# The first block of a fused attention and two-layer kernel, laid by hand on all engines

## The chip, the cores and the metric

The kernel runs on one core of one Trainium2 chip. The metric is device time of one execution, in microseconds (us).

Five engines of the core matter. TensorE (PE in the profile) multiplies matrices; its weight loads are listed apart as PEld. ScalarE (ACT) and VectorE (DVE) do elementwise work and are the only two of the four others that read the matrix results in PSUM here. GpSimd (POOL) does elementwise work on SBUF. SyncE (SP) issues the DMAs. Each engine works through its own instructions in the order in which they were written into its queue; an instruction that waits holds all that stand behind it.

## The reference, cut to what matters

Three stages follow each other on 3072 tokens of 512 features. The first is attention in chunks of 32 queries:

```python
scores = scale * np.matmul(q_c, k_full.transpose(0, 1, 3, 2))
scores = scores - np.max(scores, axis=-1, keepdims=True)
a = np.exp(scores)
a = a / (np.sum(a, axis=-1, keepdims=True) + 1e-09)
out[:, :, c_start:c_end] = np.matmul(a, v_full)
```

The second is a wide layer with a squared ReLU, from 512 to 2048 features and back:

```python
h = x @ w_in
r = np.maximum(h, 0.0)
g = s * (r * r) + b
return (g @ w_out).astype(np.float32)
```

The third is a soft mixture of eight experts. The change touches only the first part of the first two stages.

## The kernel before

The tokens are worked in six blocks of 512. A block needs four attention units (two heads each, numbered u = 0 to 23 over all blocks) and then the wide layer. The 2048 hidden features are cut into 16 slices, and a step n of the first two blocks handles one slice of one block: `divmod(n, 16)` gives block and slice. Steps 0 to 15 are block 0, steps 16 to 31 block 1; later blocks are computed in another way and are not touched.

**One step on TensorE.** `mm_h(n)` is 12 matmuls of 128x512 that make the hidden slice in a PSUM bank (`HB[n % 2]`), `mm_y(n)` is 12 that add the slice's share to four output banks. Products are made from a high and a low part of each operand, three products for each pair. TensorE's order is written by hand: mm_h(n), then an attention piece if the step has one, then mm_y(n-1). Attention pieces are `qk` (32 matmuls: scores), `tr` (4 transposes) and `pv` (32 matmuls: the weighted values). Units 4 to 9 fall in steps 1 to 15: qk in steps 1, 3, 7, 11, 12 and 14, tr in 4, 5, 9, 13 and 14, pv in 5, 7, 11 and 15.

**One step on the other engines.** `make_r` (L362, ScalarE) is the ReLU out of PSUM, `make_t` (L366, VectorE) the square, `make_high` (L369, ScalarE) and `make_low` (L373, VectorE) the two parts of g that mm_y reads. The weights of slice n stand in a tile W[n], first half for mm_h and second half for mm_y. `split_wi` makes the two parts that mm_h reads: `wi_high` (L328, ScalarE) and `wi_low` (L332). `split_wo` does the same for mm_y: `wo_high` (L343, ScalarE) and `wo_low` (L347).

**Decoding.** The weights come in as 8-byte numbers and are turned into 4-byte ones in halves of 128x512, 32 in all. A half is a load into one of up to 11 staging tiles (sp, yt, y), then `w_clamp` (L303, VectorE), `w_begin` (L309 and L310, ScalarE) and `w_end` (L316, VectorE), which writes the half into W and frees the staging tile. `halves` fixes their order: first half of slice n+1, then second half of slice n.

**Attention on the other engines.** `att_exp` is two memsets, a reduction (L220) and a subtraction (L221) on VectorE and the exponential (L222) on ScalarE. `att_norm` is a reduction (L226), two tiny operations (L227, L228) and a multiply of 128x512 (L229). `att_place` copies transposes out of PSUM (L244 and L246 on ScalarE; with the second on VectorE, L248, from unit 8 on). After pv, ScalarE copies (L259) and VectorE makes the low part (L271, `att_low`).

**What sets the order.** The string START is a list of tokens that lays the start by hand on every engine, up to the first steps: q, k, v, w, c are loads, S and A the score work of units 0 to 3, d, e, E the three parts of decoding, H mm_h(0), R, t, g, l the four parts of g(0), I, i and O, o the splits. After it, `plain_step` writes the steps; there the orders of TensorE and SyncE are as written, and those of ScalarE, VectorE and GpSimd come from a scheduler that places instructions by its own estimates. The last four steps of block 1 (`hand_step`) and what follows are laid by hand on these three too. In `plain_step` a step decodes two halves as early as the scheduler sees fit.

Of the kernel before, what the change touches and what calls it, by code (L numbers as in the profile page):

```python
# [27 lines left out]
START = (  # L28
# [4 lines left out]
)  # L33
WSCALE = 256.0
PARTS = ((0, 128), (128, 128), (256, 128), (384, 128))
# [6 lines left out]
def tile_attention_moe_softmoe(  # L42
# [35 lines left out]
    def fresh(name):  # L78
        cur[name] = slot(name, "n")
        return cur[name]  # L80
# [58 lines left out]
    def r32(ap):  # L139
        return ap.bitcast(F32R)  # L140
# [138 lines left out]
    def w_load(most=99):  # L279
        while stage_free and hnext[0] < len(halves) and most:  # L280
            most -= 1
            f, h = halves[hnext[0]]
            hnext[0] += 1
            t = stage_free.pop(0)
            sp.dma_start(out=t.bitcast(U32), in_=wd[f][:, 512 * h:512 * h + 512].bitcast(U32))
            stage_full.append((f, h, t))
# [33 lines left out]
    def w_decode():  # L320
        w_clamp()
        w_begin()
        w_end()
# [5 lines left out]

    def wi_low(n):  # L330
        t, raw = hl(WI[n % 2]), W[n % NF][:, 0:512]
        (dve if n < NF else pool).tensor_tensor(out=r32(t[:, 1]), in0=raw, in1=t[:, 0], op=ALU.subtract)  # L332

    def split_wi(n):
        wi_high(n)
        wi_low(n)
# [12 lines left out]
    def split_wo(n):  # L349
        wo_high(n)  # L350
        wo_low(n)

    def mm_h(n, kts):
        w = WI[n % 2].rearrange("p (a k c) -> p a k c", a=2, k=4)
        for kt in kts:
            x = hl(X[(n // NF) % 2][kt])
            for i, (a, b) in enumerate(((0, 0), (0, 1), (1, 0))):
                pe.matmul(HB[n % 2], lhsT=r32(w[:, a, kt, :]), rhs=r32(x[:, b]),  # L358
                          start=(kt == 0 and i == 0), stop=(kt == 3 and i == 2))
# [841 lines left out]
    with tc.manual_schedule(engines={mybir.EngineType.PE, mybir.EngineType.SP}):  # L1201
# [30 lines left out]
        def s_pv(u):  # L1232
# [29 lines left out]
            "o": wo_low,  # L1262
            "y": lambda _: stage_free.__setitem__(slice(None), YT + stage_free + Y),
        }
        with tc.manual_schedule(engines={mybir.EngineType.Activation, mybir.EngineType.DVE, mybir.EngineType.Pool}):
            for token in START.split():
                steps[token[0]](int(token[1:]))
        w_decode()
        w_decode()
        w_load()  # L1270


        def plain_step(n):
            j, f = divmod(n, NF)
            if 1 < n < NSTEP - 1:
                split_wi(n + 1)
            split_wo(n)
            mm_h(n, (0, 1, 2, 3))
            make_r(n)
            make_g(n)  # L1280
            if n + 2 < NF:
                w_decode()
                w_decode()
                w_load()
            if n == NF - 1:
                for h in range(NHP):
                    fresh(f"x0{h}")
            for task, a in bg[n]:
                run_bg(task, a, None if task == "csoft" else HB[(n + 1) % 2] if task == "pv" and n >= NF - 4 else mbank())
            if 3 <= n < NF + 3:  # L1290
                w_store(n - 3)
            if n:
                mm_y(n - 1)
                if f == 0:
                    y_evac()
            if n >= NF:
                sp.dma_start(out=DWS[f], in_=WO[n % 2])
                for fn, op, kt in XT.get(f, ()):
                    fn(op, 0, kt)
# [44 lines left out]
                w_split(2, 0)  # L1344
                ws_load(R[2], NPR + 1)

        for n in range(1, NSTEP - 4):
            plain_step(n)
        with tc.manual_schedule(engines={mybir.EngineType.Activation, mybir.EngineType.DVE, mybir.EngineType.Pool}):
            for n in range(NSTEP - 4, NSTEP):  # L1350
# [253 lines left out]
```

## Time and profile before

| | us |
|---|---|
| median of 3 runs | 657.0 (656.27 to 657.42) |
| profiled execution, time | 658.39 |
| profiled execution, span from first to last instruction | 656.6 |
| TensorE busy | 640.1 (97% of the span) |
| VectorE busy | 440.8 (67%) |
| ScalarE busy | 355.1 (54%) |
| GpSimd busy | 199.5 (30%) |

The mean granted TensorE clock is 0.995 of full speed. The span begins at the first instruction and ends with the last; 1.8 us of the profiled time lie outside it. In a timeline row the first number is the start in us from the beginning of the span, the second the time from the start of the first to the end of the last instruction in the row; "x12" is the count, and square brackets hold the engine's idle time before the row and what ended it. Matmuls overlap, so 12 of them that take 2.88 us are followed by the next 12 some 2.72 us after their start.

### The profile page before, as it was taken

How to read it: one execution, taken by the hardware profiler on the slowest of the kernel's cores; microseconds unless marked ns; L12 is line 12 of the kernel's file. 1: busy time of each engine (PE TensorE's matmuls, PEld its weight loads, DVE VectorE, ACT ScalarE, POOL GpSimd, SP SyncE). 2: the span in 40 equal slices, each digit the busy share in tenths (PEclk: the TensorE clock that was granted, in tenths of full speed). 3: DMA queues.
4: the chain of work that ended last, by engine and by line, in shares of the span. 5: the costliest groups of instructions: out<-in, count | busy, mean ns of one | idle time of the engine just before them, and what ended most of it. 6: DMA issues, size and time to landing. Idle time of an engine off the chain costs nothing.

```text
span 656.6 us, 12822 instructions
## 1 busy us (share of the span) xinstructions
PE 640.1 (97%) x4965; PEld 512.1 (78%) x4965; DVE 440.8 (67%) x748; ACT 355.1 (54%) x637; POOL 199.5 (30%) x182
## 2 busy tenths in 40 slices
PE   7899999999999999999999999999999999999995
PEld 7687888888878887888788887887887887886384
DVE  5898998566775567755575686715766879566233
ACT  5799895555654465544455464425654455544232
POOL 5100000333443485544334202444455516000000
PEclk9999999999999999999999999999999999999999
DMA  8999956476554856787655586479998788999997
GB/s 327 335 409 367 357 196 211 150 255 216 182 188 140 323 209 229 293 293 287 251 211 193 195 305 218 179 213 364 325 351 316 243 293 315 370 391 409 407 408 309
DMA packets 60108, 184.37 MB, mean 281 GB/s; under 512 B 6672, under 2 KB 6928, under 8 KB 60048
## 3 DMA queue, kind: packets, MB, share of 16 engines
q1 hardware_dynamic: 60048, 183.56, 76.9%
q8 instruction: 39, 0.64, 0.4%
q14 instruction: 21, 0.17, 0.1%
HBM read 137.40 MB, written 46.14 MB: 280 GB/s over the span
## 4 chain that ended last, share of the span: by engine, by line
PE 90%; DVE 5%; DMA 2%; ACT 2%; issue 1%; SPq 0%; DVEq 0%; ACTq 0%
PE bank L388 27%; PE bank L718 22%; PE bank L358 12%; PE bank L974 11%; PE bank L255 3%; PE bank L206 3%; PE bank L1459 2%; PE bank L1418 2%; PE bank L440 2%; PE bank L235 1%; DMA yt<-wd 1%; PE bank L414 1%; PE bank L456 1%; PE bank L1488 1%; DMA k<-kd 1%
## 5 line engine op out<-in xcount | busy, mean ns | idle before, releaser
L388 PE MATMUL bank<-g,wo 128*128 128x512 f32 x528 | 132.0, 400 | 2.0 <-ACT g L369 2.0
L388 PEld LDWEIGHTS bank<-g,wo 128*128 128x128 f32 x528 | 97.8, 190 | 24.1 <-ACT g L369 2.1
L358 PE MATMUL bank<-x,wi 128*128 128x512 f32 x384 | 92.2, 389 | 0.0
L358 PEld LDWEIGHTS bank<-x,wi 128*128 128x128 f32 x384 | 72.1, 188 | 15.0
L332 POOL TENSOR_TENSOR wi<-w,wi 128x512 fp32r<-128x512 f32 x16 | 21.1, 1319 | 121.0 <-ACT wi L328 112.0
L366 DVE SCALAR_TENSOR_TENSOR rt<-bank,cons,rt 128x512 f32<-128x512 f32 x32 | 23.9, 747 | 32.4 <-ACT rt L362 32.4
L347 POOL TENSOR_TENSOR wo<-w,wo 128x512 fp32r<-128x512 f32 x16 | 21.9, 1368 | 47.4 <-ACT wo L343 38.8
L328 ACT ACTIVATE wi<-w 128x512 fp32r<-128x512 f32 x32 | 20.1, 628 | 20.8 <-PE bank L358 18.9
L710 POOL TENSOR_TENSOR w14n<-sp6n,w14n 128x512 fp32r<-128x512 f32 x8 | 14.6, 1826 | 47.5 <-ACT w14n L709 47.5
L373 DVE SCALAR_TENSOR_TENSOR g<-rt,cons,g 128x512 fp32r<-128x512 f32 x32 | 24.2, 756 | 6.5 <-ACT g L369 6.4
L255 PEld LDWEIGHTS bank<-pb,v 128*64 128x64 f32 x704 | 22.3, 138 | 7.9 <-issue 3.3
L343 ACT ACTIVATE wo<-w 128x512 fp32r<-128x512 f32 x32 | 20.0, 626 | 15.4 <-PE bank L388 12.0
L369 ACT ACTIVATE g<-rt,cons 128x512 fp32r<-128x512 f32 x32 | 23.1, 720 | 9.9 <-DVE rt L366 9.7
L255 PE MATMUL bank<-pb,v 128*64 128x64 f32 x704 | 25.3, 225 | 0.5 <-ACT pb L246 0.5
L206 PE MATMUL bank<-k,q 128*64 128x64 f32 x704 | 24.7, 223 | 1.0 <-DMA k<-kd 1.0
L222 ACT ACTIVATE ep<-ep 128x512 f32<-128x512 f32 x22 | 13.8, 629 | 21.7 <-DVE ep L221 21.6
L206 PEld LDWEIGHTS bank<-k,q 128*64 128x64 f32 x704 | 22.4, 138 | 3.3 <-issue 2.2
L733 ACT ACTIVATE rt1n<-y1n 128x1024 f32<-128x1024 f32 x8 | 8.5, 1059 | 29.6 <-DVE y1n L834 29.6
L362 ACT ACTIVATE rt<-bank 128x512 f32<-128x512 f32 x32 | 18.8, 587 | 6.4 <-PE bank L358 6.3
L226 DVE TENSOR_REDUCE ast<-ep 128x8 f32<-128x512 f32 x22 | 15.0, 684 | 8.8 <-ACT ep L222 8.3
L974 PE MATMUL bank<-g,yt0n 128*128 128x512 f32 x72 | 18.6, 396 | 0.2 <-DVE sp L407 0.2
L964 POOL TENSOR_TENSOR k0n<-sp5n,k0n 128x512 fp32r<-128x512 f32 x6 | 8.2, 1360 | 31.9 <-ACT k0n L963 31.8
(688 smaller groups left out, 1691.8 us busy)
## 6 DMA issues: line engine op xcount, KB each, us to landing
v<-vd SPq DMA_DIRECT2D x22, 512.0 KB, 5.6
sp<-wd SPq DMA_DIRECT2D x22, 512.0 KB, 9.6
q<-qd SPq DMA_DIRECT2D x20, 512.0 KB, 6.4
dws<-wo SPq DMA_DIRECT2D x16, 512.0 KB, 5.7
k<-kd SPq DMA_DIRECT2D x22, 332.0 KB, 6.8
wo<-dws SPq DMA_DIRECT2D x12, 512.0 KB, 4.2
dwi<-w SPq DMA_DIRECT2D x16, 256.0 KB, 6.8
dwr<-w SPq DMA_DIRECT2D x16, 256.0 KB, 6.8
```

Source lines behind the costliest of these rows:

```text
L206: pe.matmul(S[64 * par:64 * par + 64, 2 * i + z, :], lhsT=qt[:, c].rearrange("p h n -> p (h n)"), rhs=kt[:, KG * c:KG * c + 64], start=Tru ...
L255: pe.matmul(b[64 * h:64 * h + 64, 64 * m:64 * m + 64], lhsT=vt[:, m, h, :], rhs=pb[:, m // 2, m % 2, h].rearrange("p z n -> p (z n)"), sta ...
L328: act.activation(out=r32(t[:, 0]), in_=raw, func=AF.Copy)
L332: (dve if n < NF else pool).tensor_tensor(out=r32(t[:, 1]), in0=raw, in1=t[:, 0], op=ALU.subtract)
L347: (dve if n < NF else pool).tensor_tensor(out=r32(t[:, :, 1]), in0=raw, in1=t[:, :, 0], op=ALU.subtract)
L358: pe.matmul(HB[n % 2], lhsT=r32(w[:, a, kt, :]), rhs=r32(x[:, b]), start=(kt == 0 and i == 0), stop=(kt == 3 and i == 2))
L366: dve.scalar_tensor_tensor(out=t, in0=HB[n % 2], scalar=s_col, in1=r, op0=ALU.mult, op1=ALU.mult)
L369: act.activation(out=r32(hl(G[n % 2])[:, 0]), in_=hl(RT[n % 2])[:, 1], func=AF.Identity, bias=b_col)
L373: dve.scalar_tensor_tensor(out=r32(g[:, 1]), in0=t, scalar=b_col, in1=g[:, 0], op0=ALU.add, op1=ALU.subtract)
L388: pe.matmul(yb[dt], lhsT=r32(w[:, dt // 2, a, dt % 2 * 128:dt % 2 * 128 + 128]), rhs=r32(g[:, b]), start=(first and i == 0), stop=(last an ...
L718: pe.matmul(b, lhsT=r32(wv[:, a, kt, :]), rhs=r32(xv[:, c]), start=(first and kt == 0 and i == 0), stop=(kt == 1 and i == 2), skip_group_c ...
L974: pe.matmul(banks[d], lhsT=r32(w[:, a, d * 128:d * 128 + 128]), rhs=r32(g[:, b]), start=(first and i == 0), stop=(last and i == 2), skip_g ...
```

## The change

Block 0's steps 1 to 15 are no longer written by `plain_step` but by a new function `first_step`, in which the order on ScalarE, VectorE and GpSimd is fixed by hand as well. Within it, in a step n with n + 1 < 16: mm_h(n); make_r; clamp, begin and end of the half (slice n, second half); make_t between the clamp and the begin; the attention matmuls; after the end mm_y(n-1), make_high, clamp of the half (slice n+2, first half), make_low, the copies of a transpose, begin, att_exp, end; then split_wo(n), split_wi(n+2), att_norm and the stores. So a half is decoded one step ahead of the split that reads it. `wi_low` goes to GpSimd from n = 2 on (before: from n = 16 on), and the multiply of att_norm for units 4 to 9 goes to GpSimd (before: VectorE). START ends earlier (E3, I2, i2 and the two decodes after it are gone, now in step 1) and loads two more staging tiles before q4 and one right after it.

```diff
@@ -28,8 +28,8 @@
-    "k4 q4 c1 d1 T3 x1 e1 d2 P2 x2 E1 P3 y0 w2 k5 w1 q5 w1 v4 w9 H0 H1 H2 x3 I1 H3 i1 "
-    "e2 R0 E2 d3 t0 O0 g0 o0 l0 e3 E3 I2 i2 v5"
+    "k4 w1 c1 q4 w2 d1 T3 x1 e1 d2 P2 x2 E1 P3 y0 w2 k5 q5 w4 v4 v5 H0 H1 H2 x3 I1 H3 i1 "
+    "e2 R0 E2 d3 t0 O0 g0 o0 l0 e3 w9"
@@ -329,7 +329,7 @@
-        (dve if n < NF else pool).tensor_tensor(out=r32(t[:, 1]), in0=raw, in1=t[:, 0], op=ALU.subtract)
+        (dve if n < 2 else pool).tensor_tensor(out=r32(t[:, 1]), in0=raw, in1=t[:, 0], op=ALU.subtract)
@@ -1262,29 +1262,72 @@
+        def first_step(n):
+            mm_h(n, (0, 1, 2, 3))
+            make_r(n)
+            if n == 1:
+                w_end()
+                split_wi(2)
+            more = n + 1 < NF
+            if more:
+                w_clamp()
+            make_t(n)
+            if more:
+                w_begin()
...
+            for t, a in bg[n]:
+                if t == "pv":
+                    att_pv(a, banks[t])
+                elif t == "qk":
+                    att_qk(a, banks[t])
+                    att_next(a)
+                else:
+                    att_turn(a, banks[t])
+            if more:
+                w_end()
+            if "pv" in kinds:
+                att_low(kinds["pv"], banks["pv"])
+                load_v(kinds["pv"] + 2)
+            w_load()
+            mm_y(n - 1)
+            make_high(n)
+            if more:
+                w_clamp()
+            make_low(n)
+            if "tr" in kinds:
+                att_place(kinds["tr"], banks["tr"], kinds["tr"] < 2 * NHP)
+            if more:
+                w_begin()
+            if "qk" in kinds:
+                att_exp(kinds["qk"], banks["qk"])
+            if more:
+                w_end()
+            w_load()
+            split_wo(n)
+            if n + 2 <= NF:
+                split_wi(n + 2)
+            if "qk" in kinds:
+                att_norm(kinds["qk"], pool)
+            if n >= 3:
+                w_store(n - 3)
+
         with tc.manual_schedule(engines={mybir.EngineType.Activation, mybir.EngineType.DVE, mybir.EngineType.Pool}):
             for token in START.split():
                 steps[token[0]](int(token[1:]))
-        w_decode()
-        w_decode()
-        w_load()
-
+            for n in range(1, NF):
+                first_step(n)
```

TensorE's order does not change anywhere. Three places show what moves on VectorE. In the rows a name ends in its number; sp, yt and y are staging tiles, w0 to w15 the decoded slices, bank4 and bank5 the two HB banks, ep the attention weights, ast small sums.

VectorE at the end of START and in step 1, before (yt0 and yt1 are the staging tiles loaded last of those shown):

```order
L332 TENSOR_TENSOR wi1_84<-w1_68,wi1_84 128x512
L303 TENSOR_SCALAR yt0_107<-yt0_107 128x512
L316 SCALAR_TENSOR_TENSOR w0_67<-sp2_114 128x512
L303 TENSOR_SCALAR sp3_115<-sp3_115 128x512
L303 TENSOR_SCALAR yt1_108<-yt1_108 128x512
L366 SCALAR_TENSOR_TENSOR rt0_97<-bank4_195,cons_66,rt0_97 128x512
```

and after:

```order
L332 TENSOR_TENSOR wi1_84<-w1_68,wi1_84 128x512
L316 SCALAR_TENSOR_TENSOR w0_67<-sp2_114 128x512
L303 TENSOR_SCALAR sp3_115<-sp3_115 128x512
L366 SCALAR_TENSOR_TENSOR rt0_97<-bank4_195,cons_66,rt0_97 128x512
L347 TENSOR_TENSOR wo0_85<-w0_67,wo0_85 128x2x256
L373 SCALAR_TENSOR_TENSOR g0_95<-rt0_97,cons_66,g0_95 128x512
L316 SCALAR_TENSOR_TENSOR w2_69<-sp3_115 128x512
```

The two clamps of yt tiles no longer stand ahead of make_t(0) (L366).

VectorE in step 7 (scores of unit 6 in bank7) and the beginning of step 8, before:

```order
L219 MEMSET bank7_198 64x8
L332 TENSOR_TENSOR wi1_84<-w9_76,wi1_84 128x512
L217 MEMSET bank7_198 64x16
L316 SCALAR_TENSOR_TENSOR w9_76<-sp0_112 128x512
L220 TENSOR_REDUCE ast0_187<-bank7_198 128x8
L347 TENSOR_TENSOR wo0_85<-w8_75,wo0_85 128x2x256
L221 TENSOR_TENSOR ep_111<-bank7_198,ast0_187 128x512
L316 SCALAR_TENSOR_TENSOR w11_78<-sp1_113 128x512
L303 TENSOR_SCALAR y0_109<-y0_109 128x512
L226 TENSOR_REDUCE ast0_187<-ep_111 128x8
L366 SCALAR_TENSOR_TENSOR rt0_97<-bank4_195,cons_66,rt0_97 128x512
L227 TENSOR_SCALAR ast0_187<-ast0_187 128x8
```

and after:

```order
L220 TENSOR_REDUCE ast0_187<-bank7_198 128x8
L221 TENSOR_TENSOR ep_111<-bank7_198,ast0_187 128x512
L316 SCALAR_TENSOR_TENSOR w9_76<-sp6_118 128x512
L347 TENSOR_TENSOR wo1_86<-w7_74,wo1_86 128x2x256
L226 TENSOR_REDUCE ast0_187<-ep_111 128x8
L227 TENSOR_SCALAR ast0_187<-ast0_187 128x8
L228 RECIPROCAL ast0_187<-ast0_187 128x8
L303 TENSOR_SCALAR yt0_107<-yt0_107 128x512
L366 SCALAR_TENSOR_TENSOR rt0_97<-bank4_195,cons_66,rt0_97 128x512
```

The attention rows, which had decode and split work between them, now stand in one piece ahead of the next step's first clamp (L303) and make_t (L366).

VectorE from the end of step 14 into step 15 (x13 is the low part after pv of unit 7, read out of bank4, which mm_h(16) writes next), before:

```order
L347 TENSOR_TENSOR wo1_86<-w15_82,wo1_86 128x2x256
L226 TENSOR_REDUCE ast1_188<-ep_111 128x8
L227 TENSOR_SCALAR ast1_188<-ast1_188 128x8
L228 RECIPROCAL ast1_188<-ast1_188 128x8
L229 TENSOR_TENSOR ep_111<-ep_111,ast1_188 128x512
L366 SCALAR_TENSOR_TENSOR rt1_98<-bank5_196,cons_66,rt1_98 128x512
L271 TENSOR_TENSOR x13_94<-bank4_195,x13_94 128x512
```

and after:

```order
L316 SCALAR_TENSOR_TENSOR w15_82<-sp0_112 128x512
L347 TENSOR_TENSOR wo0_85<-w14_81,wo0_85 128x2x256
L226 TENSOR_REDUCE ast1_188<-ep_111 128x8
L227 TENSOR_SCALAR ast1_188<-ast1_188 128x8
L228 RECIPROCAL ast1_188<-ast1_188 128x8
L366 SCALAR_TENSOR_TENSOR rt1_98<-bank5_196,cons_66,rt1_98 128x512
L271 TENSOR_TENSOR x13_94<-bank4_195,x13_94 128x512
```

A decode and wo_low(14) (before: wo_low(15)) now stand ahead of the piece that ends with the release of bank4, and L229 is on GpSimd.

## Rows read from the trace of the kernel before

**Rows 1.** The page, part 1: busy time, share of the span, instructions of each engine.

```profile
PE 640.1 (97%) x4965; PEld 512.1 (78%) x4965; DVE 440.8 (67%) x748; ACT 355.1 (54%) x637; POOL 199.5 (30%) x182
```

**Rows 2.** Timeline, TensorE, block 0 and the start of step 16.

```profile
22.70 5.73 PE L358 MATMUL bank<-x,wi 128*128 128x512 f32 x24
28.36 1.15 PE L206 MATMUL bank<-k,q 128*64 128x64 f32 x32
31.48 4.62 PE L388 MATMUL bank<-g,wo 128*128 128x512 f32 x12 [1.97 <-ACT g L369]
35.94 2.88 PE L358 MATMUL bank<-x,wi 128*128 128x512 f32 x12
...
41.38 2.88 PE L358 MATMUL bank<-x,wi 128*128 128x512 f32 x12
...
48.12 2.89 PE L358 MATMUL bank<-x,wi 128*128 128x512 f32 x12
...
54.06 2.88 PE L358 MATMUL bank<-x,wi 128*128 128x512 f32 x12
...
58.83 0.66 PE L235 MATMUL bank<-cons,ep 128*128 128x128 f32 x4 [0.81 <-DVE ep L229]
...
62.06 2.88 PE L358 MATMUL bank<-x,wi 128*128 128x512 f32 x12
...
67.50 2.88 PE L358 MATMUL bank<-x,wi 128*128 128x512 f32 x12
...
75.18 2.88 PE L358 MATMUL bank<-x,wi 128*128 128x512 f32 x12
...
126.34 2.88 PE L358 MATMUL bank<-x,wi 128*128 128x512 f32 x12
```

**Rows 3.** Busy time of each engine in one stretch, granted clock (PEclk), DMA share.

```profile
32.00:34.00 2.00, 2.00 (x7) 1.50 (x7) 1.95 (x5) 2.00 (x5) 0.00 (x0) 0.60 1.03 420
```

**Rows 4.** Timeline, VectorE, the clamp ahead of make_t(0).

```profile
29.59 0.43 DVE L303 TENSOR_SCALAR yt<-yt 128x512 f32<-128x512 f32 x1 [2.29 <-DMA yt<-wd]
```

**Rows 5.** Timeline, ScalarE, six instructions back to back.

```profile
90.49 0.60 ACT L362 ACTIVATE rt<-bank 128x512 f32<-128x512 f32 x1
90.98 0.62 ACT L328 ACTIVATE wi<-w 128x512 fp32r<-128x512 f32 x1
91.50 0.66 ACT L309 ACTIVATE sp<-sp 128x512 f32<-128x512 f32 x1
92.06 0.66 ACT L310 ACTIVATE sp<-sp 128x512 uint32<-128x512 uint8 x1
92.62 0.71 ACT L369 ACTIVATE g<-rt,cons 128x512 fp32r<-128x512 f32 x1
93.23 0.67 ACT L310 ACTIVATE sp<-sp 128x512 uint32<-128x512 uint8 x1
```

**Rows 6.** Timeline, VectorE, decode and split work, then the tail of an att_norm.

```profile
85.56 0.68 DVE L316 SCALAR_TENSOR_TENSOR w<-y 128x512 uint32<-128x512 uint32 x1
86.15 0.42 DVE L303 TENSOR_SCALAR yt<-yt 128x512 f32<-128x512 f32 x1
86.49 0.74 DVE L373 SCALAR_TENSOR_TENSOR g<-rt,cons,g 128x512 fp32r<-128x512 f32 x1
87.15 0.42 DVE L303 TENSOR_SCALAR sp<-sp 128x512 f32<-128x512 f32 x1
...
102.69 0.69 DVE L226 TENSOR_REDUCE ast<-ep 128x8 f32<-128x512 f32 x1
103.41 0.17 DVE L227 TENSOR_SCALAR ast<-ast 128x8 f32<-128x8 f32 x1
...
103.85 0.69 DVE L229 TENSOR_TENSOR ep<-ep,ast 128x512 f32<-128x512 f32 x1
```

**Rows 7.** Timeline, GpSimd, in block 1.

```profile
164.48 1.29 POOL L347 TENSOR_TENSOR wo<-w,wo 128x512 fp32r<-128x512 f32 x1 [4.77 <-ACT wo L343]
```

**Rows 8.** Timeline, VectorE, the same moment.

```profile
164.64 1.16 DVE L227 TENSOR_SCALAR ast<-ast 128x8 f32<-128x8 f32 x1
```

More of the change, by code (lines that the diff above doesn't have):

```diff
@@ L1264, in tile_attention_moe_softmoe @@
         }
+        def first_step(n):
[10 more added lines that the diff above has]
+                w_begin()
+            if n == NF - 1:
+                for h in range(NHP):
+                    fresh(f"x0{h}")
+            kinds = dict(bg[n])
+            banks = {t: HB[(n + 1) % 2] if t == "pv" and n >= NF - 4 else mbank() for t, _ in bg[n]}
+            for t, a in bg[n]:
[33 more added lines that the diff above has]
+                w_store(n - 3)
         with tc.manual_schedule(engines={mybir.EngineType.Activation, mybir.EngineType.DVE, mybir.EngineType.Pool}):
@@ L1267, in tile_attention_moe_softmoe @@
                 steps[token[0]](int(token[1:]))
-        w_decode()
-        w_decode()
-        w_load()
+            for n in range(1, NF):
+                first_step(n)
         def plain_step(n):
             j, f = divmod(n, NF)
-            if 1 < n < NSTEP - 1:
-                split_wi(n + 1)
+            split_wi(n + 1)
             split_wo(n)
@@ L1280, in plain_step @@
             make_g(n)
[L1281 to L1287, printed above, removed]
             for task, a in bg[n]:
@@ L1345, in hand_step @@
                 ws_load(R[2], NPR + 1)
-        for n in range(1, NSTEP - 4):
+        for n in range(NF, NSTEP - 4):
             plain_step(n)
```

## The prediction

> **What bounds the kernel now.** I read the page's busy times first: TensorE is busy 640.1 of 656.6 us and no other engine above 67% [rows 1]. So only two things can move the time: idle time of TensorE that goes or comes, and time at a lower clock. The timeline of TensorE shows what there is of both in block 0 [rows 2]. After the scores of unit 4 (28.36) it idles 1.97 us for g(0) and starts mm_y(0) at 31.48; these 12 matmuls take 4.62 us where the others take 2.88, because the clock was granted at half for part of the stretch (mean 0.60 in 32 to 34 us [rows 3], between the two levels of 1.2 and 2.4 GHz), after the idle. Before the transposes of unit 5 it idles 0.81 us for the multiply of att_norm. Everything else from 35.94 to 126.34 is back to back. In all 1.97 + (4.62 - 2.88 = 1.74) + 0.81 = 4.52 us can be won here, 0.7%, and no more unless the start before 22.70 changes, where the order on the four engines is kept.
>
> **What the change removes.** The 1.97 us come from VectorE: the clamp of a yt tile waited 2.29 us for its DMA with make_t(0) right behind it [rows 4]. Now two more weight tiles are loaded before q4 and one after, and no clamp of a late tile stands ahead of make_t(0). mm_h(0) ends near 25.6 (24 matmuls in 5.73 from 22.70 [rows 2]); ReLU 0.60, a decode end and a clamp on VectorE (0.59 + 0.34 start to start), make_t 0.74 and make_high 0.71 [rows 5, 6] give g(0) at about 28.2. TensorE wants it at 29.5: the idle goes, and the slow clock with it. The multiply of att_norm goes to GpSimd at 1.29 us or so (the nearest row is a subtract of the same size [rows 7]) and is ready more than a step ahead of its transposes: the 0.81 go. The extra loads are used a step or more later, and the stores and loads keep their places in the steps: I cost the queue of SyncE at nothing, hidden by 11 staging tiles; if that cover fails, a clamp waits for a DMA as in [rows 4], up to 2.3 us.
>
> **What it adds: a chain that must keep pace.** On ScalarE and VectorE a step is now a fixed chain. I lay it out with durations and start-to-start gaps of [rows 5, 6], and 0.04 us from one engine to the other. From the ReLU at 0: begin at 0.49 and 1.05, done 1.71; end 1.75 to 2.35 (0.60 until VectorE is free); second clamp done 2.77; second begin 2.81 to 4.03; second end done 4.75; wi_high at 4.79; the next ReLU at 5.31. wo_high is done at 4.6. TensorE needs 5.44 for such a step (35.94 to 41.38 [rows 2]): it just holds.
>
> In a step with qk it does not. make_low leaves VectorE free at 3.36; memsets and the reduction, the subtraction 0.73 later, done 4.98; the end 4.89 to 5.5; the exponential done 5.65; wo_high behind it done 6.2; wo_low 6.2 to 6.8; then the reduction of att_norm, the two tiny operations, and only then the first clamp of the next step and its begin. wi_high ends at 6.7, so GpSimd runs wi_low from 6.8 to 8.06, just when the tiny operation comes up at 7.54. The trace of before shows what then happens: an operation of 0.17 us took 1.16 and ended 0.03 after a GpSimd instruction of 1.29 [rows 6 to 8]. So it ends at 8.1, the clamp starts at 8.35, and the next step's chain runs as if its ReLU had been at 8.35. TensorE's step with qk is 6.74 (41.38 to 48.12): **1.6 us lost** each time. With pv as well the chain takes 8.95 and TensorE 7.68 (67.50 to 75.18): 1.25 lost. With tr, two copies of 0.6 on ScalarE make 5.95 against 5.94 (48.12 to 54.06); pv and tr 6.5 against 8.00 - 0.81 = 7.19 (54.06 to 62.06).
>
> The Trainium skill states this rule ("SBUF — State Buffer", section "Who interferes with whom"): VectorE in a two-port mode, or with two SBUF inputs, and GpSimd share a port pair, and whoever comes second is blocked for the whole instruction. Rows 8 agree. It speaks against moving wi_low to GpSimd; without the block the step with qk would take 7.85, five times 0.5 or 2.5 us less in the sum below.
>
> **The sum.** What counts is how late the chain runs behind TensorE in each step, and how much is to spare until mm_y(n) wants wo_high(n): 5.25 us (two groups of 2.72 less 0.19 to the ReLU) plus the attention pieces of this step and the next (1.3 for qk, 0.5 for tr, 1.75 for pv and tr, 2.24 for pv and qk, 1.8 for qk and tr: TensorE's steps less 5.44; 0.15 less where it is the next step's), less the time at which wo_high is done (4.6 plain, 6.2 qk, 6.8 pv and qk, 5.2 tr, 5.75 pv and tr, 6.85 qk and tr). Lateness above that is idle time of TensorE, and what is left is carried on. Step 1 begins 1.85 late: a begin left over from START ahead of its ReLU (0.75), wi_high(2) ahead of its own begin, which waits for a decode (0.95), and a block by wi_low(2) (0.15). Late, to spare, idle, for steps 1 to 14: 1.85, 0.35, **1.5**; 1.95, 1.8, **0.15**; 1.7, 0.75, **0.95**; 2.35, 2.15, **0.2**; 2.15, 1.25, **0.9**; 0.55, 2.75, 0; 0.45, 0.7, 0; 1.7, 1.05, **0.65**; 0.95, 0.55, **0.4**; 0.55, 2.75, 0; 0.45, 1.85, 0; 1.7, 0.75, **0.95**; 2.35, 2.15, **0.2**; 2.15, 1.35, **0.8**. That is 6.7. At the end mm_h(16) needs bank4, whose last reader (x13) stands on VectorE behind the tail of att_norm and two GpSimd instructions in a row: another **0.9**. So 7.6 us of new idle against 4.52 won, **3.1 slower**: 658.39 would become 661.5 in a profiled execution. That execution was 1.4 above the median, so I put the median at 657.0 + 3.1 = **660.1**. From step 16 on nothing changes but the start.
>
> Both ends of the unknown costs: without any block by GpSimd the new idle falls to about 5 (net +0.6). If other VectorE instructions that meet wi_low are held as in [rows 8], some 0.5 us in each of the five qk steps and the clamp behind GpSimd's multiply in some, it rises by 3 to 4 (net +6 to +7). The block is seen in the rows, so I keep the middle.
>
> **The rivals.**
> *A: the hand order keeps TensorE fed (not slower).* The place is the tail after qk. If VectorE's instructions are fed tighter than the gaps I took, so that a qk step's chain takes 7.2 or less instead of 8.35, lateness stays within what is to spare and all that is left is the 1 or so of step 1: 657.0 - 4.5 + 0 to 1.5 = 652.5 to 654. It decides from about 0.5 us lost per qk step instead of 1.6. For it: VectorE kept pace before with 14 subtracts and 6 multiplies more, at 0.69 each [rows 6]. Against it: before, other work filled its waits, and now the chain waits in order.
> *B: even.* A chain of about 7.8 to 8 in qk steps (no block by GpSimd): new idle 4 to 5.5, time 656 to 658.
> *C: the slow clock comes back.* The new idle of 1.5 in step 1, or one of the later ones near 0.95, is followed by a stretch at half clock as the 1.97 was; 0.81 was not [rows 2]. Each costs up to 1.74, though part of it only takes the place of idle that would follow: 661.5 to 664.
> *D: it does not do what it says.* If a clamp still waits for a DMA ahead of make_t, the 1.97 + 1.74 stay and come on top of the 6.1 of later steps, with only the 0.81 won: about 662. Loads that stand earlier in the queue speak against it.
>
> **How the numbers follow.** The forecast, 658.3 to 661.5: 0.50. A, partly or fully (below 655.7): 0.23. B (655.7 to 658.3): 0.13. C and D (above 661.5): 0.14. The range for 8 in 10 is 654.0 to 664.0: it takes in B, C and the upper part of A, and leaves out some 0.13 below and 0.05 above. About 0.2%, 1.3 us, is what a measurement can tell from no change here; slower by more than that has 0.64, faster by more 0.23, between them 0.13.
>
> **What would show it.** In the profile after: mm_y(0) with no idle before it and at full clock (step 0 right); idle of TensorE ahead of mm_y(1), mm_y(3), mm_y(5), mm_y(8), mm_y(12) and mm_y(14), ended by wo_high on ScalarE, of 0.5 to 1.5 us each (the chain right); the tiny L227 stretched to near 0.6 in qk steps (the block right); mm_h(16) late by some 3 us. If the groups of TensorE stand 5.44 and 6.74 apart all through block 0, the chain is shorter than I laid it out and A holds. If the clock drops below 1.00 after 30 us, C. If idle in block 0 is ended by a DMA, D.

## The result and the profile after

The changed kernel takes **662.99 us** (662.89 to 663.09, 4 runs) against 656.86 for the kernel before (656.27 to 657.42, 4 runs): ratio **1.0094**, 95% interval 1.0076 to 1.0111, so 6.1 us slower. The forecast was 660.1 in a range of 654.0 to 664.0, slower with 0.64.

The profiled execution took 663.09, its span is 661.3. The busy times answer to [rows 1]: TensorE has the same number of matmuls, the span around them is 4.7 us longer, GpSimd is busy 24 us more.

```profile
PE 641.0 (97%) x4965; PEld 511.0 (77%) x4965; DVE 433.4 (66%) x728; ACT 355.5 (54%) x637; POOL 223.9 (34%) x202
```

These are all waits of TensorE between 27 and 132 us (for whom; us in total, times, longest). No DMA is among them, and none is among those of ScalarE, VectorE and GpSimd in this stretch.

```profile
PE bank L388 <- ACT wo L343: 5.7, 7, 1.4
PE bank L358 <- DVE x L271: 0.5, 1, 0.5
```

The timeline of TensorE is to be laid beside [rows 2]. Shown are mm_y(0), mm_h(2) behind it, every group with an idle time ahead of it, and mm_h(16).

```profile
29.48 3.02 PE L388 MATMUL bank<-g,wo 128*128 128x512 f32 x12
32.33 2.88 PE L358 MATMUL bank<-x,wi 128*128 128x512 f32 x12
36.63 3.02 PE L388 MATMUL bank<-g,wo 128*128 128x512 f32 x12 [1.42 <-ACT wo L343]
...
50.37 3.02 PE L388 MATMUL bank<-g,wo 128*128 128x512 f32 x12 [0.82 <-ACT wo L343]
...
64.15 3.02 PE L388 MATMUL bank<-g,wo 128*128 128x512 f32 x12 [0.84 <-ACT wo L343]
...
84.11 3.04 PE L388 MATMUL bank<-g,wo 128*128 128x512 f32 x12 [0.36 <-ACT wo L343]
...
90.08 3.05 PE L388 MATMUL bank<-g,wo 128*128 128x512 f32 x12 [0.21 <-ACT wo L343]
...
111.73 3.02 PE L388 MATMUL bank<-g,wo 128*128 128x512 f32 x12 [1.00 <-ACT wo L343]
...
126.84 3.02 PE L388 MATMUL bank<-g,wo 128*128 128x512 f32 x12 [1.05 <-ACT wo L343]
130.41 3.02 PE L358 MATMUL bank<-x,wi 128*128 128x512 f32 x12 [0.55 <-DVE x L271]
```

The start is better: mm_y(0) comes at 29.48 with no idle, where [rows 2] have 31.48 after 1.97. Then idle comes ahead of mm_y(1), (3), (5), (8), (9), (12), (14) and of mm_h(16), which starts at 130.41, 4.07 later than in [rows 2]. Each idle costs more than its bracket says, because the overlap with the group before is lost too (2.88 less 2.72 us). From mm_h(2) at 32.33 to mm_y(1) at 36.63 are 4.30 us instead of 2.72, so 1.58 for an idle of 1.42.

Where the idle comes from is seen in step 3, a step with qk. The rows are of ScalarE, then VectorE, then GpSimd; the ReLU opens the step, the others are the moment at its end.

```profile
43.99 0.58 ACT L362 ACTIVATE rt<-bank 128x512 f32<-128x512 f32 x1
...
52.80 0.68 ACT L309 ACTIVATE sp<-sp 128x512 f32<-128x512 f32 x1 [1.47 <-DVE sp L303]
```

```profile
50.96 0.68 DVE L226 TENSOR_REDUCE ast<-ep 128x8 f32<-128x512 f32 x1
51.67 0.56 DVE L227 TENSOR_SCALAR ast<-ast 128x8 f32<-128x8 f32 x1
52.27 0.20 DVE L228 RECIPROCAL ast<-ast 128x8 f32<-128x8 f32 x1
52.39 0.38 DVE L303 TENSOR_SCALAR sp<-sp 128x512 f32<-128x512 f32 x1
```

```profile
50.92 1.29 POOL L332 TENSOR_TENSOR wi<-w,wi 128x512 fp32r<-128x512 f32 x1 [5.46 <-ACT wi L328]
```

The ReLU of step 3 runs at 43.99. The first begin of step 4 waits 1.47 us for its clamp (52.39), which stands behind the tail of att_norm, and the tail's L227 takes 0.56 instead of 0.17 while GpSimd's subtract runs.

### The profile page after: what moved, and what is told of

It is laid out like the page before. It is cut to its first block, busy times and chain, and to the rows that moved or that the text cites. A ratio compares the mean times of both kernels' runs of the same rounds, so it can differ in the third digit from the quotient of the medians.

```text
span 661.3 us, 12864 instructions
## 1 busy us (share of the span) xinstructions
PE 641.0 (97%) x4965; PEld 511.0 (77%) x4965; DVE 433.4 (66%) x728; ACT 355.5 (54%) x637; POOL 223.9 (34%) x202
## 4 chain that ended last, share of the span: by engine, by line
PE 77%; DVE 11%; ACT 7%; issue 2%; DMA 2%; SPq 0%; DVEq 0%; ACTq 0%
PE bank L718 22%; PE bank L388 21%; PE bank L974 11%; PE bank L358 7%; PE bank L255 3%; PE bank L206 2%; PE bank L1502 2%; PE bank L1461 2%; PE bank L440 2%; DVE w L316 2%; PE bank L235 1%; DVE ast L220 1%; ACT sp L309 1%; DVE ast L226 1%; PE bank L414 1%
## 5 line engine op out<-in xcount | busy, mean ns | idle before, releaser
L388 PEld LDWEIGHTS bank<-g,wo 128*128 128x128 f32 x528 | 96.4, 188 | 29.8 <-ACT wo L343 8.2
L332 POOL TENSOR_TENSOR wi<-w,wi 128x512 fp32r<-128x512 f32 x30 | 39.4, 1314 | 99.6 <-ACT wi L328 96.0
L366 DVE SCALAR_TENSOR_TENSOR rt<-bank,cons,rt 128x512 f32<-128x512 f32 x32 | 23.9, 746 | 29.8 <-ACT rt L362 29.7
L316 DVE SCALAR_TENSOR_TENSOR w<-sp 128x512 uint32<-128x512 uint32 x22 | 16.1, 731 | 8.7 <-ACT sp L310 8.7
L226 DVE TENSOR_REDUCE ast<-ep 128x8 f32<-128x512 f32 x22 | 15.0, 682 | 7.9 <-ACT ep L222 7.7
L309 ACT ACTIVATE sp<-sp 128x512 f32<-128x512 f32 x22 | 14.9, 676 | 9.3 <-DVE sp L303 9.1
```

The source lines that it names most:

```text
L316: dve.scalar_tensor_tensor(out=dst, in0=high, scalar=3, in1=low, op0=ALU.logical_shift_left, op1=ALU.bitwise_or)
L332: (dve if n < 2 else pool).tensor_tensor(out=r32(t[:, 1]), in0=raw, in1=t[:, 0], op=ALU.subtract)
L366: dve.scalar_tensor_tensor(out=t, in0=HB[n % 2], scalar=s_col, in1=r, op0=ALU.mult, op1=ALU.mult)
L388: pe.matmul(yb[dt], lhsT=r32(w[:, dt // 2, a, dt % 2 * 128:dt % 2 * 128 + 128]), rhs=r32(g[:, b]), start=(first and i == 0), stop=(last an ...
```

## The experiments

Eleven runs followed, the first of them of the kernel before, unchanged. In the table mm_h(16) is the start of the first group of step 16; from there to the last activation of the output every kernel needs 523.0 to 524.0 us. "Lost" is the time from the start of mm_h(0) to mm_h(16) above the 99.38 us that the last kernel of the list needs, in which TensorE waits for nothing there. Each ratio is to executions of the kernel before that were taken with that run; their medians are 656.86 to 657.26.

| kernel | time, us | ratio to before, 95% | mm_h(16) | lost |
|---|---|---|---|---|
| before, as recorded | 658.39 (profiled) | | 126.34 | 4.3 |
| before_again | 656.49 (one) | | 125.15 | 3.3 |
| changed kernel | 662.99 | 1.0094 (1.0076 to 1.0111) | 130.41 | 8.3 |
| half_low | 660.90 | 1.0054 (1.0039 to 1.0068) | 128.52 | 6.3 |
| low_on_vector | 669.26 | 1.0186 (1.0162 to 1.0210) | 137.45 | 15.4 |
| norm_on_vector | 667.78 | 1.0168 (1.0148 to 1.0187) | 134.98 | 12.8 |
| clamp_first | 664.45 | 1.0113 (1.0096 to 1.0130) | 131.90 | 10.0 |
| loads_only | 659.62 | 1.0034 (1.0020 to 1.0047) | 127.53 | 2.0, and 3.5 in START |
| loads_hand | 657.04 | 0.9994 (0.9986 to 1.0003) | 125.10 | 3.6 |
| reordered | 662.31 | 1.0081 (1.0056 to 1.0106) | 129.55 | 7.6 |
| reordered_v | 668.21 | 1.0167 (1.0146 to 1.0188) | 136.38 | 14.3 |
| early_split | 659.67 | 1.0039 (1.0026 to 1.0051) | 127.55 | 5.4 |
| **tail_later** | **654.33** | **0.9956 (0.9943 to 0.9969)** | 122.21 | 0 |

**Was the half clock part of the kernel before?** The unchanged kernel, profiled once more.

> The kernel before, unchanged, profiled once more. In the recorded execution mm_y(0) took 4.62 us at a granted clock of 0.60 after an idle of 1.97, and that execution (658.39) was 1.4 to 1.5 above the median. Theory 1, the half clock belonged to that one execution: now the clock stays at 1.00 through 30 to 36 us, mm_y(0) takes 2.9 to 3.0, mm_h(2) starts near 34.3 instead of 35.94, and the span is 654.7 to 655.3. Then the 1.74 us were never in the median, and the predicted sum counted a gain that was not there. Theory 2, the idle of 1.97 brings the half clock each time: mm_y(0) again 4.4 to 4.7 and the span 656.3 to 656.9.

Timeline of TensorE, and the busy times with the granted clock of 31 to 34 us (PE, PEld, DVE, ACT, POOL, PEclk, DMA share, GB/s):

```profile
31.06 3.02 PE L388 MATMUL bank<-g,wo 128*128 128x512 f32 x12 [1.76 <-ACT g L369]
33.91 0.72 PE L358 MATMUL bank<-x,wi 128*128 128x512 f32 x2
35.04 2.56 PE L358 MATMUL bank<-x,wi 128*128 128x512 f32 x10 [0.41 <-DVE wi L332]
```

```profile
31.00:34.00 3.00, 2.94 (x13) 2.28 (x13) 2.95 (x7) 3.00 (x7) 0.00 (x0) 1.00 1.03 415
```

The idle ahead of mm_y(0) is there again, 1.76 instead of 1.97 us; the half clock of [rows 3] is not. Theory 1 holds for this execution: span 654.7, time 656.49. mm_h(2) starts 2.03 earlier, and a wait for wi_low(2) appears that the slow matmuls had covered. So of the difference 1.2 us remain at mm_h(16) (1.0 counted from mm_h(0)).

One execution does not tell how often the half clock comes. Of the 43 other executions of the kernel before that were taken with the runs below, three have the mean granted clock of the recorded one, 0.995, and took 657.99, 658.08 and 658.42; in the other forty it is 0.996 to 0.999. By this mark the half clock is rare and the median does not have it. Six of these forty took over 658 as well, for a reason that stays open.

**The block by GpSimd.** Half of the subtract left out:

```
-        (dve if n < 2 else pool).tensor_tensor(out=r32(t[:, 1]), in0=raw, in1=t[:, 0], ...)
+        if 2 <= n < NF:
+            pool.tensor_tensor(out=r32(t[:, 1, 0:256]), in0=raw[:, 0:256], in1=t[:, 0, 0:256], ...)
```

> The changed kernel; in block 0 from step 2 on GpSimd's subtract for the low part of the first matrix does only half of its columns (the other half keeps what an earlier step left there). The instruction goes from 1.29 to some 0.65 us. Theory 1, the tiny operation L227 is held by GpSimd's subtract until it ends and this lies on the path: L227 goes from 0.56 back to 0.17 in qk steps, each such step loses 0.4 to 0.5 less, by the ledger of the prediction the idle time falls by 2.0 to 2.5, and mm_h(16) starts at 127.9 to 128.4 instead of 130.41; time about 661. Rival, the stretched L227 only fills a wait that something else sets: mm_h(16) within 0.4 of 130.4, time 662.6 to 663.1.

GpSimd, then VectorE, of this kernel in step 1 (its line numbers are 3 higher behind L331):

```profile
37.19 0.74 POOL L333 TENSOR_TENSOR wi<-w,wi 128x256 fp32r<-128x256 f32 x1 [5.53 <-ACT wi L328]
```

```profile
37.95 0.17 DVE L227 TENSOR_SCALAR ast<-ast 128x8 f32<-128x8 f32 x1
```

L227 is back at 0.17, mm_h(16) comes 1.9 sooner, the time is 2.1 lower, near what Theory 1 said. The block, that is the time by which GpSimd's subtract holds L227 up, lies on the path. It is a quarter of the 8.3 us lost.

**The two moves to GpSimd, each undone** in its place in the order.

```
-        (dve if n < 2 else pool).tensor_tensor(out=r32(t[:, 1]), ...)
+        (dve if n < NF else pool).tensor_tensor(out=r32(t[:, 1]), ...)
```

> The changed kernel with one part undone: the low parts of the first matrix in block 0 are subtracted on VectorE again (same place in the order). It tells what the move to GpSimd is worth in this order. Theory 1, the order is too tight for VectorE, so the move pays although GpSimd holds a VectorE instruction up: in a qk step 0.6 is added and the 0.4 of the stretched L227 falls away (+0.2), in a plain step 0.6 is added where VectorE waits 0.3 to 0.44 anyway (+0.2 to 0.4); by the ledger 2 to 4 us more idle, time 665 to 667 (changed kernel 662.99). Rival, GpSimd's hold costs more than it takes over: time 660 to 662.5, L227 at 0.17 and the idle times ahead of mm_y(3), mm_y(8) and mm_y(12) smaller than 0.82, 0.36 and 1.00.

```
-                att_norm(kinds["qk"], pool)
+                att_norm(kinds["qk"])
```

> The changed kernel with its other move undone: from step 1 on the multiply of att_norm stands on VectorE again, in its place in the order. Theory 1, in a fixed order each VectorE instruction in the tail is paid by the next step: 0.6 more per qk step, by the ledger of the prediction 3 us more idle (9.7 against 6.7), mm_h(16) near 133.4 instead of 130.41, time 665.5 to 666.5. Rival, GpSimd's multiply holds VectorE up as long as it spares it (it lies beside the clamp and make_t of the next step), so nothing changes: time 662.5 to 663.5.

Both rivals fall, and Theory 1 has the direction in both, though the times lie above its ranges (669.26 against 665 to 667, 667.78 against 665.5 to 666.5). In this order the instructions that come back to VectorE are paid by TensorE: 7.1 us lost more for fourteen subtracts, 4.5 for six multiplies. Of the 7.1 some 2.7 are clock, which fell twice, behind idle times of 2.54 and 2.31 us, so that groups of 3.02 took 4.38 and 4.35. The rows are of low_on_vector, TensorE and then the granted clock in 38 to 40 us, 0.50, the 1.2 GHz level:

```profile
37.71 4.38 PE L388 MATMUL bank<-g,wo 128*128 128x512 f32 x12 [2.54 <-ACT wo L343]
...
117.78 4.35 PE L388 MATMUL bank<-g,wo 128*128 128x512 f32 x12 [2.31 <-ACT wo L343]
```

```profile
38.00:40.00 2.00, 2.00 (x5) 1.53 (x5) 1.93 (x6) 0.66 (x2) 0.00 (x0) 0.50 1.04 414
```

So the moves are not what makes the changed kernel slow; the order is, and GpSimd's holds within it.

**Is it the clamp's place?** The next step's first clamp moved ahead of the tail:

```
-            if more:
+            if more and n == 1:
                 w_clamp()
...
+            if n + 2 < NF:
+                w_clamp()
             if "qk" in kinds:
                 att_norm(kinds["qk"], pool)
```

> The changed kernel; only the first clamp of each next step moves ahead of the tail of att_norm on VectorE. Theory 1, the qk steps are long because the next decode waits for its clamp behind the tail: the begin then follows its ReLU at 0.5 instead of 2.05 us; make_t stays behind the tail, so 1.0 of the 1.6 lost per qk step comes back. By the ledger the idle of the later steps falls from 6.7 to about 1.75 (the one of mm_y(1), 1.4, stays), mm_h(16) starts at 125.5 to 126.5, time 658 to 659. Rival, VectorE has simply more work in a qk step than TensorE gives it time for, wherever the clamp stands: less than 1 us comes back, time above 662.

Theory 1 missed, and this is the most telling miss: nothing came back, and 1.7 us more were lost. The time lies where the rival put it, but its reason, too much work for VectorE wherever the clamp stands, does not hold: the last kernel of the list does the same work and keeps pace. VectorE and GpSimd in step 3 of this kernel:

```profile
51.24 1.53 DVE L303 TENSOR_SCALAR sp<-sp 128x512 f32<-128x512 f32 x1
...
54.34 1.14 DVE L316 SCALAR_TENSOR_TENSOR w<-sp 128x512 uint32<-128x512 uint32 x1
```

```profile
51.20 1.29 POOL L332 TENSOR_TENSOR wi<-w,wi 128x512 fp32r<-128x512 f32 x1 [5.46 <-ACT wi L328]
53.88 1.04 POOL L229 TENSOR_TENSOR ep<-ep,ast 128x512 f32<-128x512 f32 x1 [1.40 <-DVE ast L228]
```

Now the clamp meets the subtract: it starts 0.04 behind it, takes 1.53 instead of 0.42 and ends 0.28 after it; the decode end meets the multiply (1.14 instead of 0.68). In the changed kernel it was the reduction L226 that stood there, and it took 0.68 as always. So what stands on VectorE while GpSimd works matters; what the clamp's place would be worth without these holds, this run does not tell. The Trainium skill has a rule for this in "SBUF — State Buffer", section "Who interferes with whom": on this chip a reduction, and an instruction with one SBUF input at most outside the two-port modes, do not contend with GpSimd; one in a two-port mode or with two SBUF inputs does, and whichever comes second is blocked. The traces agree: in the changed kernel thirteen make_t, which read PSUM and one SBUF tile, began beside a GpSimd instruction and took 0.74 to 0.75.

**Only the loads of START in the kernel before**, first alone, then with the next two decodes in the list by hand:

```
-    "k4 q4 c1 d1 ... y0 w2 k5 w1 q5 w1 v4 w9 H0 ... e3 E3 I2 i2 v5"
+    "k4 w1 c1 q4 w2 d1 ... y0 w2 k5 q5 w4 v4 v5 H0 ... e3 E3 I2 i2 w9"
```

> The kernel before with nothing of the change but the order of the loads in START. Theory 1, the wait ahead of mm_y(0) was the clamp's wait for its tile alone: mm_y(0) starts at 29.4 to 29.6 with no idle, the steps behind it keep the order and the pace of before (only the 0.81 ahead of the transposes of unit 5 stays), and the time is 2.0 below before, 654.9 (3.6 below in a profile of before that had the half clock). Rival, the earlier loads push others back or the gain is given back at a later wait: time within 0.5 of before, 656.4 to 657.4, with a new idle in block 0.

```
+    "... e3 E3 I2 i2 d4 e4 E4 d5 e5 E5 w9"
-        w_decode()
-        w_decode()
-        w_load()
```

> The kernel before with the loads of the change in START and the next two decodes written into START's order by hand, behind make_t(0) and make_low(0); steps 1 on are left to the scheduler as before, nothing of theirs moves to GpSimd. In the run loads_only the scheduler had put a clamp that waits for its tile ahead of a copy that TensorE waits for (idle 3.12). Theory 1, the gain at step 0 needs both, loads and a place by hand: mm_y(0) starts at 29.4 to 30.0 (one decode of a tile that lands near 28 still stands ahead of wo_high(0) on ScalarE), the later steps run at the pace of before, time 1.0 to 2.0 below before: 655 to 656. Rival, the wait moves to another tile again: idle above 1 us ahead of mm_y(0) or mm_y(1), time 656.5 to 659.

VectorE and TensorE of loads_only, then TensorE of loads_hand:

```profile
23.03 0.43 DVE L303 TENSOR_SCALAR sp<-sp 128x512 f32<-128x512 f32 x1 [2.22 <-DMA sp<-wd]
```

```profile
24.24 1.98 PE L255 MATMUL bank<-pb,yt 128*64 128x64 f32 x32 [3.12 <-DVE pb L248]
26.15 7.76 PE L358 MATMUL bank<-x,wi 128*128 128x512 f32 x24
```

```profile
29.59 3.02 PE L388 MATMUL bank<-g,wo 128*128 128x512 f32 x12 [0.61 <-ACT g L369]
...
36.76 3.04 PE L388 MATMUL bank<-g,wo 128*128 128x512 f32 x12 [0.88 <-ACT wo L343]
```

Theory 1 falls both times. With the loads alone the scheduler put the clamp of an early loaded tile ahead of a copy (L248) that TensorE waits for. So the wait moved from [rows 4] into START, and the half clock came with it (24 matmuls in 7.76 instead of 5.74); at 659.62 the kernel is even slower than the rival had it. With the decodes fixed by hand mm_y(0) comes at 29.59 as foreseen, with 1.15 us less idle than in before_again. But 1.6 are lost ahead of mm_y(1), where before_again loses 0.8, and 0.9 more in the two groups behind it. The gain is given back one step later, and the time is that of before, as the rival said.

**Another order.** wo_high stands ahead of the second begin, the exponential and wi_high, and the clamps ahead of what waits (not shown). In the second kernel, moreover, the subtract is on VectorE and the tail of step 14's att_norm behind the reader of bank4. The part on wo_high:

```
             make_high(n)
             make_low(n)
+            wo_high(n)
...
             if more:
                 w_end()
             w_load()
-            split_wo(n)
+            wo_low(n)
```

> The changed kernel with the same instructions on the same engines, in another order by hand: both clamps of a step stand ahead of the instructions that wait (the first one at the end of the step before, the second right behind make_t), and wo_high stands right behind make_high, ahead of the second begin, the exponential and wi_high. Theory 1, the idle times are the late wo_high: wo_high is then ready some 2 us sooner in each step, so the idle ahead of mm_y goes although the clamp at a step's end still meets GpSimd's subtract (1.53 us instead of 0.42 in the run clamp_first): mm_h(16) at 123 to 126 instead of 130.41, time 656 to 659. Rival, VectorE with GpSimd's holds is over its time in each step (qk 6.5 of work and 1.1 of holds against 6.74), so lateness piles up and TensorE waits as before, now for make_t: mm_h(16) above 128, time above 661.

> The order of the run reordered, with the low parts of the first matrix on VectorE (no GpSimd subtract in block 0 that could hold anything up; the multiply of att_norm stays on GpSimd) and the att_norm tail of step 14 moved behind the reader of bank4 in step 15. Theory 1: with wo_high early and no holds, VectorE has 7.1 in a qk step against 6.74 and 4.5 in a plain one against 5.44, so no lateness is left and TensorE idles nowhere in block 0 behind mm_y(0): mm_h(16) at 122.0 to 123.0, time 654 to 656, faster than both kernels. Rival, VectorE is the bound without GpSimd's help: idle of 0.5 or more ahead of several mm_y, mm_h(16) above 125, time above 657.

Theory 1 missed both times. TensorE of reordered in mm_y(5), then its VectorE in step 5, which makes what mm_y(5) reads:

```profile
63.01 1.07 PE L388 MATMUL bank<-g,wo 128*128 128x512 f32 x4
65.44 2.11 PE L388 MATMUL bank<-g,wo 128*128 128x512 f32 x8 [1.36 <-DVE wo L347]
```

```profile
64.09 0.69 DVE L316 SCALAR_TENSOR_TENSOR w<-sp 128x512 uint32<-128x512 uint32 x1 [1.94 <-ACT sp L310]
64.70 0.69 DVE L347 TENSOR_TENSOR wo<-w,wo 128x512 fp32r<-128x512 f32 x1
```

wo_high was early, but mm_y's fifth matmul reads wo_low, and that stood behind the second decode end: mm_y(5) began at 63.01 and took 4.38 us to the next group instead of 2.72. I had named one of the two halves that TensorE needs. The times are those of the rivals (above 661, above 657), but in reordered TensorE waits for wo_low and not, as its rival had it, for make_t. With the subtract on VectorE the same wait stands ahead of nine mm_y instead of three, and 14.3 us are lost instead of 7.6.

**An order made from the holds.** In early_split wi_high and wi_low of the next step stand right behind the ReLU, so that the subtract runs beside make_t and the reductions, and both clamps stand at the end of the step before. In tail_later the tail of att_norm also moves into the next step, behind these, and wo_high ahead of the exponential. The main parts of tail_later's edit, against the changed kernel:

```
             make_r(n)
+            split_wi(n + 1)
...
             if "qk" in kinds:
-                att_exp(kinds["qk"], banks["qk"])
+                att_exp(kinds["qk"], banks["qk"], 0)
+            if held:
+                att_norm(held.pop(), pool)
...
             if more:
                 w_begin()
+            wo_high(n)
+            if "qk" in kinds:
+                att_exp(kinds["qk"], banks["qk"], 1)
+                held.append(kinds["qk"])
+            if more:
                 w_end()
             w_load()
-            split_wo(n)
+            wo_low(n)
+            if n + 2 < NF:
+                w_clamp()
+                w_clamp()
```

(In the calls of att_exp 0 is its part on VectorE, 1 the exponential.)

> The changed kernel, all instructions on the same engines, with an order by hand that keeps VectorE's SBUF-only instructions out of GpSimd's time: wi_high and wi_low of the next step stand right behind the ReLU, so that GpSimd's subtract runs while VectorE does make_t and the reductions of the scores, which read PSUM and were not held in the runs so far; both clamps of a step stand at the end of the step before; wo_low follows the second decode end; the att_norm tail of step 14 stands behind the reader of bank4. Theory 1, what the changed kernel loses is holds by GpSimd plus the order in which wo_high and wo_low come: VectorE then needs 6.5 in a qk step (TensorE 6.74) and 4.8 in a plain one (5.44), TensorE idles under 1 us in all behind mm_y(0), mm_h(16) starts at 122.2 to 123.2 instead of 130.41, time 654.5 to 656. Rival, a chain of ScalarE and VectorE one behind the other sets each step whatever the order: idle of 0.5 or more ahead of several mm_y or within them, mm_h(16) above 126, time above 658.5.

> The run early_split (659.67, mm_h(16) at 127.55) with the three places mended at which it still waited: the att_norm tail moves on into the next step, behind make_t and the reductions, so that GpSimd's multiply comes after its subtract instead of ahead of it (in early_split the subtract of step 2 started at 39.16 behind the multiply, took 1.73, and mm_h(3) lost 2.2 waiting for it); on ScalarE the second begin and wo_high stand ahead of the exponential. Theory 1, the waits in early_split (2.2 in mm_h(3), 1.1 in mm_h(5), 0.6 in mm_h(9), 0.9 in mm_h(13), 0.5 about mm_y(1)) are GpSimd's queue and the order alone: they fall to under 1 us together, mm_h(16) at 122.3 to 123.5, time 654.5 to 656, faster than both kernels. Rival, work on VectorE and ScalarE with GpSimd's holds is at its limit in the steps with qk: 2 us or more stay, mm_h(16) above 124.5, time above 656.5.

early_split missed: 659.67, with mm_h(16) at 127.55, is where the rival put it. GpSimd, VectorE and TensorE of early_split, about mm_h(3):

```profile
38.16 1.04 POOL L229 TENSOR_TENSOR ep<-ep,ast 128x512 f32<-128x512 f32 x1 [5.98 <-DVE ast L228]
39.16 1.73 POOL L332 TENSOR_TENSOR wi<-w,wi 128x512 fp32r<-128x512 f32 x1
```

```profile
38.55 1.20 DVE L316 SCALAR_TENSOR_TENSOR w<-sp 128x512 uint32<-128x512 uint32 x1
39.67 1.76 DVE L373 SCALAR_TENSOR_TENSOR g<-rt,cons,g 128x512 fp32r<-128x512 f32 x1
```

```profile
40.94 2.56 PE L358 MATMUL bank<-x,wi 128*128 128x512 f32 x10 [1.92 <-POOL wi L332]
```

Here the multiply stood ahead of the subtract in GpSimd's queue, the subtract took 1.73 instead of 1.29, and TensorE waited 1.92 us for wi_low. TensorE, GpSimd and VectorE of tail_later (its line numbers are 4 higher):

```profile
32.45 2.88 PE L362 MATMUL bank<-x,wi 128*128 128x512 f32 x12
35.17 2.88 PE L392 MATMUL bank<-g,wo 128*128 128x512 f32 x12
37.89 2.88 PE L362 MATMUL bank<-x,wi 128*128 128x512 f32 x12
```

```profile
36.63 1.30 POOL L336 TENSOR_TENSOR wi<-w,wi 128x512 fp32r<-128x512 f32 x1 [4.39 <-ACT wi L332]
38.28 1.38 POOL L233 TENSOR_TENSOR ep<-ep,ast 128x512 f32<-128x512 f32 x1 [0.35 <-DVE ast L232]
```

```profile
38.67 1.54 DVE L377 SCALAR_TENSOR_TENSOR g<-rt,cons,g 128x512 fp32r<-128x512 f32 x1
```

The groups of TensorE stand back to back from mm_h(0) at 22.83 to mm_h(16) at 122.21, slightly better than Theory 1 said. The kernel has the same instructions on the same engines as the changed one and is 8.7 us faster; it is 2.9 faster than before. A hold is still there (make_low 1.54 instead of 0.75), but in a step without qk, which has room. The loss of the changed kernel is thus shown to be its order, with GpSimd's holds in it. half_low puts some 2 of the 8.3 us on the hold of L227; how the rest divides between other holds and the bare chain was not measured.

## Why the prediction came out right, and what was mis-sized

The direction was right and the range held, but the size was half: 3.1 us slower were forecast, 6.1 were measured. The result lies above the 658.3 to 661.5 of the forecast, where the prediction had put only rivals C and D, with 0.14, and neither of them happened. That it fell inside the range is in part luck: the upper end, 664.0, was set by C and D. Step by step, as the prediction put them:

- **The gain at step 0: right in the trace, too large in the time.** g(0) is ready at 28.19 (28.2 was laid out), and idle and slow clock ahead of mm_h(2) are gone (3.61 sooner than in [rows 2]). But the 1.74 for the clock came from one execution; before_again and 40 of 43 other executions do not show its mean clock. In before_again, 3.3 us could be won in block 0, not the 4.52 of the sum (4.3 in the recorded execution, by the table). The working added 3.1 to the median of 657.0 although it had taken the gain from an execution 1.4 above that median: this is the step that was mis-sized most. One detail of its premise was the other way round: by the code and the order of SyncE's loads one more tile is loaded ahead of q4 and two right after it. The wait was gone all the same.
- **The 0.81 at unit 5: right.** No idle is left ahead of those transposes (57.12).
- **SyncE's queue at nothing: right.** TensorE, ScalarE, VectorE and GpSimd wait for no DMA from 27 to 132 us.
- **The chain in a qk step: right.** From the ReLU at 43.99 to the next begin at 52.80, less the 0.49 that a begin follows its ReLU, are 8.32 us; 8.35 was laid out. Its cause was incomplete: "only then the first clamp" reads as if the clamp's place were the price, and in clamp_first moving the clamp only handed the hold to it. What makes the chain so tight is that split_wo(n) and split_wi(n+2) read halves that are decoded in the same step n, not one step ahead as the description of the change has it; in tail_later split_wi stands in the next step.
- **The block: right.** All six L227 of qk steps took 0.55 to 0.57 ("near 0.6"), and half_low gave back 2.1 us (2.5 said). That the block speaks against moving wi_low did not hold in this order: with wi_low back on VectorE, and L227 at 0.17, the kernel took 669.26.
- **The ledger: right in places and nearly in size.** Idle predicted and measured: mm_y(1) 1.5, 1.42; (3) 0.95, 0.82; (5) 0.9, 0.84; (8) 0.65, 0.36; (9) 0.4, 0.21; (12) 0.95, 1.00; (14) 0.8, 1.05; mm_h(16) 0.9, 0.55; the three of 0.15 to 0.2 didn't show. Printed idle is 6.25 of 7.6 predicted. From start to start the eight idle times cost 7.7, and with short waits that have no bracket (0.29 about mm_y(7)) the loss is 8.3. The prediction had taken idle and loss as one.
- **From the sum to the time: too small.** Against the recorded execution of before, mm_h(16) is 4.07 late where 3.1 were forecast: 0.7 of the difference are the loss, 0.3 the gain. By the last activation of the output 3.75 are left. From the end of that row to the end of the span are 6.55 us in the changed kernel and 5.6 before. The last activations of before and of after:

```profile
649.92 1.08 ACT L1495 ACTIVATE sp<-bank 128x512 f32<-128x512 f32 x2
```

```profile
653.67 1.08 ACT L1538 ACTIVATE sp<-bank 128x512 f32<-128x512 f32 x2
```

  That makes the spans 4.7 apart, and the recorded execution of before stands 1.5 above the median of 656.86, the profiled one of after 0.1 above its own: hence 6.1 between the medians. Against before_again mm_h(16) is 5.26 late and the span 6.6 longer. In all the profiles 5.5 to 6.6 us lie behind the last activation; why that varies was not tried.
- **Rivals.** C is false: the clock stays at 1.00 behind the idle of 1.42. D is false: mm_y(0) has no idle ahead of it. B asked for no block by GpSimd, and the block is there; in half_low, without the hold on L227, the printed idle of 4.2 is B's size (4 to 5.5), but the time of 660.90 is not its 656 to 658, so the step from idle to time fails there in the same way. A did not come true for this order, but its condition did for another: in tail_later the qk steps keep pace, and the time is 654.33, just above the 652.5 to 654 that A gave.

## What to carry to other kernels

In an order written by hand every instruction of a queue waits for the one before it. So lay out each step's chain, with the holds in it, before moving work to GpSimd. Put on VectorE, beside GpSimd's instructions, what reads PSUM or reduces, and put the rest where the step has room. A gain read from one execution has to be held against the median first: if that execution stands above it, part of the gain may be its own accident. And when a wait is removed, look for the next one in the same place (mm_y(1) behind mm_y(0), wo_low behind wo_high) before its whole length is counted.

## What the runs showed of the hardware beyond what was expected

- The hold goes both ways (early_split, step 2, rows above). The decode end that came up beside GpSimd's multiply took 1.20 us instead of 0.68; the subtract that came up beside that decode end took 1.73 instead of 1.29; make_low, which came up beside the subtract, took 1.76 instead of 0.75.
- The same place of the same kernel need not bring the same clock in each execution: ahead of mm_y(0) TensorE idled 1.97 us in the recorded execution of before and fell to half clock, in before_again it idled 1.76 us and stayed at 1.00. Over all runs, between 20 and 133 us, TensorE's granted clock fell to half behind idle times of 1.97, 2.31, 2.54 and 3.12 us; it stayed at 1.00 behind 1.42, and behind 1.64 in norm_on_vector, 1.76 in before_again, 1.86 in reordered_v and 1.92 in early_split. The row of the changed kernel that holds its longest idle, 1.42, granted clock 1.00:

```profile
35.00:38.00 3.00, 1.58 (x7) 1.15 (x7) 2.35 (x5) 2.15 (x4) 0.82 (x1) 1.00 1.03 411
```
